# Dealing the second products of a two-layer network between its first products, with contiguous loads, later value loads and a factor moved into the exponent

## The chip, the cores and the metric

The kernel runs on one core of one Trainium2 chip. The metric is the device time of one execution in microseconds (us). Five engines take part: TensorE (PE; its weight loads are shown as PEld), VectorE (DVE), ScalarE (ACT), GpSimd (POOL) and SyncE (SP), which here only issues DMAs.

## The reference, cut to what matters

Blockwise causal attention for 8 batches of 8 heads, 576 tokens of 64 numbers each, then two matrix layers over the 4608 tokens. All of it is float32.

```python
scores = scale * np.matmul(q, k.transpose(0, 1, 3, 2))      # scale = 1/8
mask = block_i >= block_j                                   # blocks of 64 tokens
scores = np.where(mask, scores, -1000000000.0)
scores = scores - np.max(scores, axis=-1, keepdims=True)
attn = np.exp(scores)
attn = attn / (np.sum(attn, axis=-1, keepdims=True) + 1e-09)
x = np.matmul(attn, v)                                      # heads side by side: 4608 x 512
h = x @ w_in                                                # 512 -> 2048
g = np.maximum(0.01 * h, h)
out = g @ w_out                                             # 2048 -> 512
```

## The kernel before, in words

**Products in parts.** To keep float32 accuracy at the speed of the one-pass type float32r, an operand is split into a high part (rounded to float32r) and a low part (the rest), and three products are added: high with high, high with low, low with high. So `xh`, `xl` are the parts of x, `wih`, `wil` those of w_in, `gh`, `gl` those of g, `woh`, `wol` those of w_out. In the first heads a plain float32 product is used instead (`plain_s` for the scores, `plain_v` for the values), which takes four passes.

**Attention.** `attention(i)` makes one piece of work: a whole head for batches 1 to 7 ("full"), or for batch 0 the rows up to token 320 of a head ("lo", i = 0 to 7) and then the rest ("hi", i = 8 to 15). It loads q and k side by side into `qk_in` (two buffers) and the values into `vf`, or from batch 1 on into the one `v_stage`; forms scores in PSUM (`p_s`; in the odd lo heads `p_h`); takes masked row maxima, negated, into `nm` (L477); forms the exponents into `prow` with `nm` as the bias, and their sums (L486); divides by the sums; transposes `prow` through TensorE into `p_t` (L551) and copies it out; multiplies by the values (L603 or L613); and puts the result into `xr`. Where `plain_s` holds, q is first multiplied by the factor in place, in `qk_in` (by `copying`, L243 on ScalarE or L244 on VectorE).

**Weights.** `weight_piece` brings the 32 pieces of the two weight matrices, which arrive as 64-bit floats: a load into `raw`, two conversions, two bit operations that put a 32-bit value together in `val`, and the split into the two parts. A piece of w_out is 128 whole rows; a piece of w_in is a block of 128 columns.

**The two layers.** Tokens go in 18 chunks of 256. For each chunk the 2048 middle columns go in 8 pairs of column tiles, u = 0 to 7, so there are 144 pairs. `ffn1` makes the first products of a pair: for each of its two tiles 12 matmuls of 256 columns into `p_h[u % 2]`. Then ScalarE forms `g` from it (L719), which is split into `gh` and `gl` (two buffers each, by u % 2). `ffn2` makes the second products: for each half m of the chunk's tokens 6 matmuls of 512 columns into the accumulator `p_o[m]`. At u = 7 each accumulator is copied into the one buffer `ob` and stored.

**What sets the order.** Every step is given to `Plan.add` with the engines that could do it and their costs, a rank, and what it reads and writes. `Plan.run` plays the program through with these costs: each engine takes, of the steps whose inputs are there, the one of lowest rank. The order in which steps are taken is the program's order on each engine, and on SyncE's queue. Matmuls of one step stay together, so before the change the 12 first products of a tile are one block, and the 6 second products of a half another. The numbers at the head of the file shift ranks (`RL`: how many heads ahead q and k are loaded; `LEAD`, `LAG`: where first and second products stand among the heads; `OFF1`, `SL1`: when weight pieces are due), and `HOLD` is how long a step waits before its second-choice engine may take it. Until the first layer starts, where TensorE would rest in this play, dummy products of the identity (`fill`, L784, into `p_o`) are put in.

Of the kernel before, what the change touches and what calls it, by code (L numbers as in the profile page):

```python
# [26 lines left out]
HS = 8  # L27
SIGNS = 4
# [5 lines left out]
RL = 3.85  # L34
RP = 0.396
RB = 0.255
RT = 1.189
RV = 1.756
RX = -1.367
RN = -0.808  # L40

LEAD = 2.089
LAG = 1.994
RS = 2.992
RG = -0.004
OFF1 = 5.088
SL1 = 12.185
AHEAD = -0.653

LAT = 1550  # L50
HOLD = 167.582
# [6 lines left out]
SLOW = 8000  # L58
JOINT = 0


class Plan:
# [37 lines left out]
    def run(self):  # L100
# [123 lines left out]
def attention_ffn(ctx: ExitStack, tc: tile.TileContext, qk: bass.AP, v: bass.AP, w_in: bass.AP, w_out: bass.AP, out: bass.AP):  # L224
    nc = tc.nc
    B, H = qk.shape[0], qk.shape[1]
    DM, DFF = w_in.shape
# [65 lines left out]
    for y in range(2):  # L293
        nc.gpsimd.memset(sums[y], 1.0)
    xr = [fixed([P, ND, S], F32, "xr0"), None]
# [30 lines left out]
    def weight_piece(num, rank, f, out_side, c0):  # L326
# [31 lines left out]
        if src.dtype != F32:  # L358

            def load():  # L360
                nc.sync.dma_start(shaped(raws[k], 2 * P), src.bitcast(I32))
# [3 lines left out]
                ("ACT", act(w, True) + 70, lambda: nc.scalar.activation(val(), top(), AF.Copy, scale=2.0**-112)),  # L365
                ("DVE+", dve(w), lambda: nc.vector.tensor_scalar_mul(val(), top(), 2.0**-112)),
# [10 lines left out]
        else:  # L377

            def load():
                nc.sync.dma_start(shaped(val()), src)  # L380
# [5 lines left out]
    def attention(i):  # L386
# [25 lines left out]

        def load():
            if qa == 0:
                nc.sync.dma_start(qkt[:rows, :, :qe], qk[b, h, :rows, :, :qe])
            else:
                nc.sync.dma_start(qkt[:rows, 0, qa:qe], qk[b, h, :rows, 0, qa:qe])
                nc.sync.dma_start(qkt[:rows, 1, :ke], qk[b, h, :rows, 1, :ke])

        add([("SP", {"full": 475, "lo": 650, "hi": 1300}[kind], load)], r0 - RL, [], [qkey], lag=dma((qe - qa + ke) * rows * 4))  # L420
# [4 lines left out]
        add([("SP", 475, lambda: nc.sync.dma_start(vt(), v[b, h, :, :nv]))], r0 - RL + 0.1, [], [vkey], lag=dma(nv * P * D * 4))  # L425
# [389 lines left out]
```

## Time and profile before

| | |
|---|---|
| median of 3 runs | 1170.11 us (1169.79 to 1174.19) |
| the profiled execution | 1170.27 us |
| its span, first to last instruction | 1168.5 us |
| TensorE, share of the span | 99% |
| TensorE on the chain that ended last | 96% |
| first products begin | 50.36 us |

In the profile, rows in order of time give a start, a duration, the engine, the line, and what is written from what. A matmul's duration reaches from its start until its result is out, longer than the distance to the next start, since matmuls overlap. A float32 product of plain operands appears as two records. The table by stage gives for each stretch its length and each engine's busy time with the number of instructions in brackets. The chain that ended last is followed back from the last instruction: at each step to what released it, or to the instruction before it on its engine.

### The profile page before, as it was taken

The page shows a single profiled execution, that of the slowest core. Times are in us where ns is not written, and L with a number is a line of the kernel's source. Part 1 is how long each engine was busy: PE and PEld are TensorE (multiplying, and loading weights), DVE is VectorE, ACT ScalarE, POOL GpSimd, SP SyncE. Part 2 cuts the span into 40 slices and gives each one's busy share as a digit, 9 for nine tenths or more (in the row PEclk, how much of TensorE's full clock was granted, in tenths as well). Part 3 has the DMA queues.
Part 4 walks back from the last instruction along what each step waited for, and adds up shares of the span by engine and source line. Part 5 has one row for each costly group of instructions (what it writes and reads, how often), then busy time and mean ns, then how long its engine had stood idle before and what let it go on. Part 6 is the DMA issues. An engine that isn't in the chain of part 4 may idle for free.

```text
span 1168.5 us, 20725 instructions
## 1 busy us (share of the span) xinstructions
PE 1159.0 (99%) x7734; PEld 1053.7 (90%) x7734; DVE 622.7 (53%) x1606; ACT 649.0 (56%) x1641; POOL 432.8 (37%) x411
## 2 busy tenths in 40 slices
PE   8999999999999999999999999999999999999998
PEld 7878889899999999999999999999999999999997
DVE  6889988975555555535344555555555555200000
ACT  7888867765555555545455556565555555322222
POOL 2332444443443443434334344343343433222221
PEclk9999999999999999999999999999999999999999
DMA  7666322211212121111111111112111100000000
GB/s 225 218 220 229 124 67 79 87 62 53 71 47 70 33 70 53 66 32 60 38 45 47 50 53 65 41 51 64 52 65 52 54 29 25 2 19 3 16 19 19
DMA packets 38950, 78.16 MB, mean 67 GB/s; under 512 B 3520, under 2 KB 24000, under 8 KB 38848
## 3 DMA queue, kind: packets, MB, share of 16 engines
q1 hardware_dynamic: 38848, 76.82, 20.4%
q8 instruction: 61, 1.00, 0.3%
q14 instruction: 41, 0.34, 0.1%
HBM read 67.37 MB, written 9.44 MB: 66 GB/s over the span
## 4 chain that ended last, share of the span: by engine, by line
PE 96%; DVE 1%; DMA 1%; ACT 1%; issue 0%; SPq 0%; POOL 0%; ACTq 0%
PE p_h L712 34%; PE p_o L731 34%; PE p_t L551 9%; PE p_s L459 8%; PE p_t L613 7%; PE p_t L603 2%; PE p_s L453 2%; PE p_o L784 1%; PE p_h L453 0%; DMA qk_in<-in_qk 0%; DMA v_stage<-in_v 0%; DVE nm L477 0%; ACT prow L486 0%; DVE ptl L250 0%; DVE qs L436 0%
## 5 line engine op out<-in xcount | busy, mean ns | idle before, releaser
L712 PE MATMUL p_h<-xh,wih 128*128 128x256 f32 x1152 | 327.8, 285 | 0.0
L712 PE MATMUL p_h<-xl,wih 128*128 128x256 f32 x1152 | 321.1, 279 | 0.5 <-DVE xl L250 0.5
L712 PE MATMUL p_h<-xh,wil 128*128 128x256 f32 x1152 | 320.6, 278 | 0.0
L251 POOL TENSOR_TENSOR gl<-g,gh 128x512 fp32r<-128x512 f32 x138 | 181.1, 1312 | 298.5 <-ACT gh L240 199.2
L486 ACT ACTIVATE prow<-p_s,nm 128x192 f32<-128x192 f32 (+4 forms) x308 | 160.5, 527 | 139.7 <-DVE nm L477 137.2
L712 PEld LDWEIGHTS p_h<-xl,wih 128*128 128x128 f32 x1152 | 217.3, 189 | 8.6 <-DVE xl L250 0.8
L712 PEld LDWEIGHTS p_h<-xh,wih 128*128 128x128 f32 x1152 | 216.7, 188 | 8.1 <-issue 0.4
L712 PEld LDWEIGHTS p_h<-xh,wil 128*128 128x128 f32 x1152 | 216.9, 188 | 0.0
L719 ACT ACTIVATE g<-p_h 128x512 f32<-128x512 f32 x144 | 85.6, 595 | 213.4 <-PE p_h L712 202.1
L517 POOL TENSOR_SCALAR prow<-prow,rec 128x576 f32<-128x576 f32 (+3 forms) x121 | 88.0, 730 | 310.3 <-DVE rec L505 282.6
L731 PE MATMUL p_o<-woh,gh 128*128 128x512 f32 x576 | 183.3, 399 | 0.0
L731 PE MATMUL p_o<-woh,gl 128*128 128x512 f32 x576 | 179.4, 393 | 0.0
L731 PE MATMUL p_o<-wol,gh 128*128 128x512 f32 x576 | 179.3, 393 | 0.0
L477 DVE TENSOR_REDUCE nm<-p_s 128x1 f32<-128x192 f32 (+4 forms) x308 | 140.1, 486 | 4.7
L551 PE MATMUL p_t<-ident,prow 128*128 128x128 f32 x960 | 130.2, 273 | 1.2 <-DVE xr L592 0.5
L731 PEld LDWEIGHTS p_o<-woh,gl 128*128 128x128 f32 x576 | 108.2, 188 | 24.3
L731 PEld LDWEIGHTS p_o<-wol,gh 128*128 128x128 f32 x576 | 108.2, 188 | 23.9
L250 DVE TENSOR_TENSOR ptl<-p_t,pth 128x512 fp32r<-128x512 f32 (+1 forms) x224 | 118.8, 567 | 16.8 <-ACT pth L240 14.3
L551 PEld LDWEIGHTS p_t<-ident,prow 128*128 128x128 f32 x960 | 110.0, 141 | 12.6 <-issue 1.9
L592 DVE TENSOR_TENSOR xr<-p_t,xr 64x64 f32<-64x64 f32 x112 | 50.2, 449 | 126.8 <-ACT xr L240 121.6
L240 ACT CAST pth<-p_t 128x384 fp32r<-128x384 f32 (+3 forms) x190 | 86.1, 499 | 39.8 <-PE p_t L551 39.6
L251 POOL TENSOR_TENSOR kl<-qk_in,kh 128x576 fp32r<-128x576 f32 x55 | 85.3, 1551 | 22.5 <-ACT kh L240 17.9
(78 smaller groups left out, 1561.7 us busy)
## 6 DMA issues: line engine op xcount, KB each, us to landing
qk_in<-in_qk SPq DMA_DIRECT2D x56, 576.0 KB, 3.7
v_stage<-in_v SPq DMA_DIRECT2D x56, 160.0 KB, 2.2
out<-ob SPq DMA_DIRECT2D x35, 256.0 KB, 2.3
raw<-in_w_in SPq DMA_DIRECT2D x16, 512.0 KB, 4.6
raw<-in_w_out SPq DMA_DIRECT2D x16, 512.0 KB, 3.9
qk_in<-in_qk SPq DMA_DIRECT2D x8, 320.0 KB, 4.0
qk_in<-in_qk SPq DMA_DIRECT2D x8, 288.0 KB, 3.7
vf<-in_v SPq DMA_DIRECT2D x8, 160.0 KB, 3.2
```

The lines of the kernel that those rows point to most:

```text
L240: one = lambda: nc.scalar.copy(dst(), src())
L250: ("DVE+" if sb else "DVE", dve(n), lambda: nc.vector.tensor_sub(dst(), one(), two())),
L251: ("POOL", pool2(n), lambda: nc.gpsimd.tensor_sub(dst(), one(), two())),
L459: go = lambda ap=ap, cols=cols, kk=kk, k0=k0, k1=k1, first=first, last=last: nc.tensor.matmul(ap, qs[z][:, cols], kk[:, k0:k1], start=firs ...
L477: [("DVE", dve(kw[t]), lambda t=t, ap=ap, flat=flat: nc.vector.tensor_reduce(nm[z][: qn[t], t : t + 1], ap[: qn[t]], axis=AX.X if flat els ...
L486: nc.scalar.activation(o, ap[: qn[t]], AF.Exp, bias=nm[z][: qn[t], t : t + 1], scale=1.0, accum_out=sums[z][: qn[t], t : t + 1])
L517: ("POOL", pool1(kw[t]), lambda: nc.gpsimd.tensor_scalar(p(), p(), by, 1.0, op0=ALU.mult, op1=ALU.mult)),
L551: return 27, lambda: nc.tensor.transpose(p_t[x][:, c : c + n], row(t, n, j * P, P), ident[:n, :n])
L613: nc.tensor.matmul(to, vs[z][:, j, :], src, start=start, stop=stop)
L712: nc.tensor.matmul(hh[:, i, :], w[:, d, f * P : (f + 1) * P], x[:, d, :], start=k == 0, stop=k == len(terms) - 1)
L719: add([("ACT", act(512), lambda: nc.scalar.activation(g, hh, AF.Prelu, alpha=0.01))], rank, [("h", z)], ["g"])
L731: nc.tensor.matmul(p_o[m], a[:, i, m * P : (m + 1) * P], w[:, 2 * u + i, :], start=u == 0 and k == 0, stop=u == NU - 1 and k == 5,)
```

## The change

1. **Second products dealt.** From u = 2 on, `ffn1` no longer makes a block of 12 first products. It takes the second products of pair u - 2 of the same chunk and deals them in: one second product, two first products, and so on. Tile i of the pair goes with half m = i. Each tile is two steps of 9 matmuls. Pairs 0 and 1 have their first products alone, and at u = 7 `ffn2` adds the second products of pairs 6 and 7, undealt.
2. **The plan.** A matmul step that depends on another matmul step no longer waits in the plan for that one's end.
3. **Contiguous loads.** w_in is laid out on the host so that a piece is 128 whole rows of 4 KB. q and k of batch 0 come from an array of their own, `qk0`, in which the columns of a lo or hi piece stand side by side, so each needs one load with one run per partition.
4. **Later value loads.** They get rank `r0 - RL + VD` with VD = 5.23, about 0.57 heads ahead of their head instead of 3.75.
5. **Factor in the exponent.** With `plain_s`, q is not multiplied. The exponent takes the factor as its `scale`, and the negated maxima in `nm` are multiplied by it, in one small step per group of rows.
6. **Choices.** The conversion of a weight's top word may run on GpSimd. HS goes from 8 to 7, so one hi head forms its scores from parts. The table of ranks, and HOLD, have other values.

```diff
-HS = 8
+HS = 7
-RL = 3.85
+RL = 5.803
...
-HOLD = 167.582
+HOLD = 62.559
...
+VD = 5.23
...
-                at = max([0] + [ends[d][1] + self.SYNC.get((ends[d][0], e), 0) for d in self.ops[i][2]])
+                at = max([0] + [ends[d][1] + self.SYNC.get((ends[d][0], e), 0) for d in self.ops[i][2] if (ends[d][0], e) != ("PE", "PE")])
...
-            src = w_in[c0 : c0 + WIDE, fs].rearrange("(c p) f -> p c f", p=P)
+            src = w_in[f, :, c0 : c0 + WIDE]
...
+                ("POOL", pool1(w), lambda: nc.gpsimd.tensor_scalar(val(), top(), 2.0**-112, 1.0, op0=ALU.mult, op1=ALU.mult)),
...
-        add([("SP", 475, lambda: nc.sync.dma_start(vt(), v[b, h, :, :nv]))], r0 - RL + 0.1, [], [vkey], lag=dma(nv * P * D * 4))
+        add([("SP", 475, lambda: nc.sync.dma_start(vt(), v[b, h, :, :nv]))], r0 - RL + VD, [], [vkey], lag=1.5 * dma(nv * P * D * 4))
...
-            add(copying(qe - qa, lambda: q_in, lambda: q_in, by=scale / 2), rp, [], [qkey])
...
+            if plain_s:
+                ts = sorted(t for t, _, _ in tiles)
+                some = nm[z][:, ts[0] : ts[-1] + 1]
+                add([
+                    ("DVE+", 75, lambda some=some: nc.vector.tensor_scalar_mul(some, some, scale / 2)),
+                    ("ACT", 110, lambda some=some: nc.scalar.activation(some, some, AF.Copy, scale=scale / 2)),
+                ], r, [], [("nm", z, t) for t in ts])
...
-                    o, ap[: qn[t]], AF.Exp, bias=nm[z][: qn[t], t : t + 1], scale=1.0, accum_out=sums[z][: qn[t], t : t + 1]
+                    o, ap[: qn[t]], AF.Exp, bias=nm[z][: qn[t], t : t + 1], scale=scale / 2 if plain_s else 1.0, accum_out=sums[z][: qn[t], t : t + 1]
...
+    def ffn1(c, u, rank, rank0):
+        z = u % 2
+        mate = u - 2 if u >= 2 else None
         for i in range(2):
...
+            one = ffn1_terms(u, i)
+            if mate is None:
+                add([("PE", one)], rank + i / 1000, xkeys + wkeys[("wi", 2 * u + i)], [("h", z)])
+                continue
+            two = ffn2_terms(mate, i)
+            for y in range(2):
+                a, b = one[6 * y : 6 * y + 6], two[3 * y : 3 * y + 3]
+                mixed = [x for k in range(3) for x in (b[k], a[2 * k], a[2 * k + 1])]
+                add(
+                    [("PE", mixed)], rank + i / 1000 + y / 2000,
+                    xkeys + wkeys[("wi", 2 * u + i)] + ffn2_keys(mate), [("h", z), ("o", i)], kind="long",
                 )
...
     def ffn2(c, u, rank):
         for m in range(2):
+            if u == NU - 1:
+                for x in (u - 1, u):
+                    add([("PE", ffn2_terms(x, m))], rank + m / 1000 + (x - u) / 300, ffn2_keys(x), [("o", m)], kind="long")
```

On TensorE, in the middle of the program, the end of a block of first products (`p_h`) and the blocks of second products (`p_o`, one accumulator for each half) behind it stand like this before (x2 is two instructions of that form):

```order
L712 MATMUL p_h_109<-xh,wih 128x256
L712 MATMUL p_h_109<-xl,wih 128x256
L712 MATMUL p_h_109<-xh,wil 128x256
L731 MATMUL p_o_110<-woh,gh_114 128x512 x2
L731 MATMUL p_o_110<-wol,gh_114 128x512 x2
L731 MATMUL p_o_110<-woh,gl_116 128x512 x2
L731 MATMUL p_o_111<-woh,gh_114 128x512 x2
L731 MATMUL p_o_111<-wol,gh_114 128x512 x2
L731 MATMUL p_o_111<-woh,gl_116 128x512 x2
```

And now, at the like place, with the last triple of one pair and the first three of the next:

```order
L733 MATMUL p_o_113<-woh,gl_117 128x512
L721 MATMUL p_h_110<-xl,wih 128x256
L721 MATMUL p_h_110<-xh,wil 128x256
L733 MATMUL p_o_112<-woh,gh_116 128x512
L721 MATMUL p_h_111<-xh,wih 128x256
L721 MATMUL p_h_111<-xl,wih 128x256
L733 MATMUL p_o_112<-woh,gh_116 128x512
L721 MATMUL p_h_111<-xh,wil 128x256
L721 MATMUL p_h_111<-xh,wih 128x256
L733 MATMUL p_o_112<-wol,gh_116 128x512
L721 MATMUL p_h_111<-xl,wih 128x256
L721 MATMUL p_h_111<-xh,wil 128x256
```

Runs of 12 first and 6 second products have become rows in which every second product stands alone between two pairs of first products.

On SyncE's queue, at the program's start, the loads of q and k (`qk_in`), values (`vf`) and weights (`raw`) before:

```order
L415 DMA qk_in_86<-in_qk 128x2x320
L425 DMA vf_130<-in_v 128x256
L415 DMA qk_in_87<-in_qk 128x2x320
L425 DMA vf_131<-in_v 128x256
L361 DMA raw_123<-in_w_in 128x4x256
```

And now:

```order
L425 DMA qk_in_86<-in_qk 128x640
L425 DMA qk_in_87<-in_qk 128x640
L432 DMA vf_132<-in_v 128x256
L432 DMA vf_133<-in_v 128x256
L363 DMA raw_125<-in_w_in 128x1024
```

Both loads of q and k have moved ahead of the values, and each has one run per partition.

On ScalarE, at the program's start, with the factor on q (L243), a weight's conversions (L365, L368) and the exponents (L486), before:

```order
L243 ACT_TABLE_LOAD
L243 ACTIVATE qk_in_86<-qk_in_86 128x320
L243 ACTIVATE qk_in_87<-qk_in_87 128x320
L365 ACTIVATE val_126<-raw_123 128x512
L368 ACTIVATE raw_123<-raw_123 128x512
L486 ACTIVATE prow_2_75,sums_98<-p_s,nm_96 128x320
```

And now, with other line numbers (L367 and L371 are the conversions, L499 the exponents):

```order
L367 ACT_TABLE_LOAD
L367 ACTIVATE val_128<-raw_125 128x512
L499 ACTIVATE prow_2_75,sums_98<-p_s,nm_96 128x320
L499 ACTIVATE prow_1_74,sums_98<-p_s,nm_96 128x192
L499 ACTIVATE prow_0_73,sums_98<-p_s,nm_96 64x64
L371 ACTIVATE raw_125<-raw_125 128x512
```

The two instructions that multiplied q are gone; one conversion now runs ahead of the first exponents instead of two. Until the first products of the layers, TensorE's order has 64 dummy products where it had 59. On ScalarE, counted to its first `g`, 8 instructions on `qk_in` are gone, 8 on `nm` have come, and conversions of a weight's top word are 6 instead of 10; GpSimd has 6 of these conversions ahead of its first `gl`.

More of the change, by code (lines that the diff above doesn't have):

```diff
@@ L32 @@
 VALS = 3
-RL = 3.85
[L35 to L48, printed above, removed]
+RL = 5.803
+RP = 0.25
+RB = 0.531
+RT = 1.509
+RV = 1.966
+RX = -3.191
+RN = -0.618
+LEAD = 2.353
+LAG = 2.006
+RS = 1.957
+RG = -0.335
+OFF1 = 4.843
+SL1 = 10.955
+AHEAD = -1.469
 LAT = 1550
-HOLD = 167.582
+HOLD = 62.559
 FILL = 235
@@ L379, in load @@
             def load():
-                nc.sync.dma_start(shaped(val()), src)
+                nc.sync.dma_start(val(), src)
             add([("SP", 475, load)], rank - AHEAD, [], [v_key], lag=dma(w * P * 4))
@@ L453, in scores @@
                     go = lambda ap=ap, cols=cols, k0=k0, k1=k1, first=first, last=last: nc.tensor.matmul(
-                        ap, qkt[:rows, 0, cols], qkt[:rows, 1, k0:k1], start=first, stop=last
+                        ap, q_in[:, cols.start - qa : cols.stop - qa], k_in[:, k0:k1], start=first, stop=last
                     )
@@ new lines, in ffn2_terms, with go @@
+    def ffn2_terms(u, m):
+        z = u % 2
+        terms = [(a, w, i) for a, w in ((gh[z], woh), (gh[z], wol), (gl[z], woh)) for i in range(2)]
+        def go(k):
+            a, w, i = terms[k]
+            nc.tensor.matmul(
+                p_o[m], a[:, i, m * P : (m + 1) * P], w[:, 2 * u + i, :],
+                start=u == 0 and k == 0, stop=u == NU - 1 and k == 5,
+            )
+        return [(RATE * DM, lambda k=k: go(k)) for k in range(6)]
+    xkeys = [(a, d) for a in ("xh", "xl") for d in range(0, CH, BLK)]
@@ L718, in ffn1 @@
         rank += RG
-        add([("ACT", act(512), lambda: nc.scalar.activation(g, hh, AF.Prelu, alpha=0.01))], rank, [("h", z)], ["g"])
+        add([("ACT", act(512), lambda: nc.scalar.activation(g, p_h[z], AF.Prelu, alpha=0.01))], rank, [("h", z)], ["g"])
         add(copying(512, lambda: gh[z], lambda: g), rank, ["g"], [("gh", z)])
@@ L723, in ffn2 @@
     def ffn2(c, u, rank):
-        z = u % 2
         for m in range(2):
-            terms = [(a, w, i) for a, w in ((gh[z], woh), (gh[z], wol), (gl[z], woh)) for i in range(2)]
-            def go(k, m=m, terms=terms):
-                a, w, i = terms[k]
-                nc.tensor.matmul(
-                    p_o[m], a[:, i, m * P : (m + 1) * P], w[:, 2 * u + i, :],
-                    start=u == 0 and k == 0, stop=u == NU - 1 and k == 5,
-                )
-            add(
-                [("PE", [(RATE * DM, lambda k=k, go=go: go(k)) for k in range(6)])], rank + m / 1000,
-                [("gh", z), ("gl", z)] + wkeys[("wo", 2 * u)] + wkeys[("wo", 2 * u + 1)], [("o", m)], kind="long",
-            )
+            if u == NU - 1:
+                for x in (u - 1, u):
+                    add([("PE", ffn2_terms(x, m))], rank + m / 1000 + (x - u) / 300, ffn2_keys(x), [("o", m)], kind="long")
             if u == NU - 1:
```

60 lines of the change are left out of this document (36 added, 24 removed).

## The prediction

> **What bounds the kernel now.** The profile's page was read first: engines, slices, chain. Then a table by stage, then rows in order of time.
>
> ```profile
> span 1168.5 us, 20725 instructions
> PE 1159.0 (99%) x7734; PEld 1053.7 (90%) x7734; DVE 622.7 (53%) x1606; ACT 649.0 (56%) x1641; POOL 432.8 (37%) x411
> PEclk9999999999999999999999999999999999999999
> PE 96%; DVE 1%; DMA 1%; ACT 1%; issue 0%; SPq 0%; POOL 0%; ACTq 0%
> L712 PE MATMUL p_h<-xh,wih 128*128 128x256 f32 x1152 | 327.8, 285 | 0.0
> L731 PE MATMUL p_o<-woh,gh 128*128 128x512 f32 x576 | 183.3, 399 | 0.0
> ```
>
> TensorE carries 96% of the chain, at full granted clock, and the largest groups have no idle time before them. The mean of one instruction (285 and 399 ns) is no price: matmuls overlap, so I price by the distance between starts. There are three groups like the first and three like the second: 144 column pairs make 3456 first products of 256 columns and 1728 second products of 512. One second and two first products, a triple, are the unit below; there are 1728 triples.
>
> Busy time by stage (TensorE, weight loads, VectorE, ScalarE, GpSimd, then clock and DMA share):
>
> ```profile
> 0.00:50.00 50.00, 46.76 (x285) 38.48 (x286) 36.38 (x107) 39.84 (x113) 9.85 (x26) 1.00 0.71 223
> 50.00:250.00 200.00, 197.49 (x1297) 173.12 (x1296) 174.34 (x418) 159.18 (x385) 85.84 (x83) 1.00 0.41 132
> 250.00:1010.00 760.00, 760.00 (x5159) 701.89 (x5158) 403.25 (x1068) 411.14 (x1078) 303.31 (x277) 1.00 0.16 51
> ```
>
> From 250 us on TensorE never rests and VectorE and ScalarE are half idle: there only the spacing of matmuls can move the time. Before 50 us no product of the layers has run; ScalarE (80%), VectorE (73%) and the loads (0.71) set the pace, and TensorE fills its waits with dummy products. The chain of this stage and the group of the dummies:
>
> ```profile
> 2.08 5.09 DMA qk_in<-in_qk
> 7.20 0.48 ACT qk_in L243
> 7.72 2.40 PE p_h L453 x6
> 46.51 1.98 PE p_o L784 x16
> ...
> 50.36 1.42 PE p_h L712 x12
> L784 PE MATMUL p_o<-ident 128*128 128x128 f32 x117 | 18.5, 308 | 1.4 <-POOL ident masks.py:199 1.4
> ```
>
> **The dealing of second products.** How matmuls follow one another now, in the tail, where attention is over:
>
> ```profile
> 1037.20 0.62 PE L731 MATMUL p_o<-woh,gl 128*128 128x512 f32 x2
> 1037.66 0.28 PE L712 MATMUL p_h<-xh,wih 128*128 128x256 f32 x1
> 1037.77 0.28 PE L712 MATMUL p_h<-xl,wih 128*128 128x256 f32 x1
> 1037.89 0.28 PE L712 MATMUL p_h<-xh,wil 128*128 128x256 f32 x1
> 1038.01 0.28 PE L712 MATMUL p_h<-xh,wih 128*128 128x256 f32 x1
> 1038.13 0.28 PE L712 MATMUL p_h<-xl,wih 128*128 128x256 f32 x1
> 1038.25 0.28 PE L712 MATMUL p_h<-xh,wil 128*128 128x256 f32 x1
> ...
> 1038.93 0.28 PE L712 MATMUL p_h<-xh,wil 128*128 128x256 f32 x1
> 1039.04 0.62 PE L731 MATMUL p_o<-woh,gh 128*128 128x512 f32 x2
> 1039.50 0.62 PE L731 MATMUL p_o<-wol,gh 128*128 128x512 f32 x2
> ```
>
> Second products are 0.46/2 = 230 ns apart. The twelve first products take 1039.04 - 1037.66 = 1.38 us, 115 ns each, but not evenly: the first five after a second product take 0.59 us (118 ns each), and the six from 1038.25 to 1038.93 take 0.68 us (113 ns each). A triple costs 230 + 2 x 115 = 460 ns.
>
> In a dealt row every first product stands within two of a second product, so the fast steps deep in a run are not reached. I take the first three steps of the run, 1037.66 to 1038.01, 117 ns each: 230 + 2 x 117 = 464 ns. Only pairs 2 to 7 of a chunk are dealt: 18 chunks x 6 pairs x 12 = 1296 triples. The term is 1296 x 4 ns = +5.2 us.
>
> Its ends: downwards, both first products at the 113 ns of the deep run, 230 + 226 = 456 ns, -5.2 us. Upwards, another run of before, which never left the slow spacing:
>
> ```profile
> 500.00 0.28 PE L712 MATMUL p_h<-xl,wih 128*128 128x256 f32 x1
> ...
> 502.00 0.63 PE L731 MATMUL p_o<-woh,gh 128*128 128x512 f32 x2
> 502.46 0.63 PE L731 MATMUL p_o<-wol,gh 128*128 128x512 f32 x2
> 502.93 0.62 PE L731 MATMUL p_o<-woh,gl 128*128 128x512 f32 x2
> ```
>
> Seventeen first products in 2.00 us are 118 ns each, and the second products behind them 0.93/4 = 232 ns. With the largest step of the fast run (1038.01 to 1038.13, 120 ns) a triple is 232 + 240 = 472 ns: +15.6 us. The middle value is nearest to the rows where the two kinds meet.
>
> The Trainium skill, page "TensorE: Matmul & The Clock Gate", section "Back-to-back issue gap", gives columns / 2.4 + about 2.5 ns between matmuls, 109 and 216 ns here, and the part on loading the stationary operand says that loading the next weights takes no read bandwidth from the running matmul. By that an undisturbed triple would be 434 ns. The rows above contradict it in both kinds; it is a rival below.
>
> The moved instructions issue no DMA. In each dealt block a wait for the halves of g now holds first products behind it. They are two pairs old by then, some 24 triples or 11 us, against one activation, one copy and one subtraction of about 0.6, 0.6 and 1.3 us:
>
> ```profile
> L719 ACT ACTIVATE g<-p_h 128x512 f32<-128x512 f32 x144 | 85.6, 595 | 213.4 <-PE p_h L712 202.1
> L251 POOL TENSOR_TENSOR gl<-g,gh 128x512 fp32r<-128x512 f32 x138 | 181.1, 1312 | 298.5 <-ACT gh L240 199.2
> ```
>
> So I price it at nothing; were half a pair late by 1 us in each of the 108 dealt pairs, it would cost 108 us, which is why the wait's cover matters. At a chunk's end in the tail the next chunk's first dealt row follows the last second products at once, and the accumulator of the second half is free only after the first half's copy, its store, and a second copy through the same `ob`:
>
> ```profile
> L240 ACT COPY ob<-p_o x33: 577/587/594, 145.0 to 1163.4; 128x512 f32<-128x512 f32 x33
> DMA to landing us min/median/max: 2.0/2.3/4.2
> ```
>
> The store starts about 0.6 us before the last second product ends, lands 2.3 us after it is issued, and the copy takes 0.6 us: some 2.7 us in all with the issue, against 6 triples x 464 = 2.8 us of cover. I take +0.2 us at each of four chunk ends, +0.8 us (0 to +4 by the slowest landing).
>
> **The first 50 us.** The factor on q is gone. On the chain it stood as 0.48 us, and the second head's load is now issued ahead of both value loads: I take -0.9 us (ends -0.5, the activation alone, and -2.0). In place of the factor each softmax scales the negated maxima, a column or three, between maximum and exponent. The nearest rows for the saving and for the addition:
>
> ```profile
> L243 ACT ACTIVATE qk_in<-qk_in 128x320 f32<-128x320 f32 (+1 forms) x8 | 3.6, 453 | 4.7 <-DMA qk_in<-in_qk 4.7
> L365 ACT ACTIVATE val<-raw 128x512 f32<-128x512 f32 x9 | 6.0, 664 | 1.4 <-DMA raw<-in_w_in 1.4
> L502 DVE TENSOR_SCALAR rec<-sums 128x3 f32<-128x3 f32 (+1 forms) x8 | 1.2, 156 | 0.1
> ```
>
> Eight factors of 0.45 us leave ScalarE (3.6 us), eight scalings at about 0.2 us (an estimate from the last row and a little more for ScalarE) come (1.6 us), and four conversions of a weight's top word move to GpSimd, busy for 9.9 of these 50 us (2.7 us). Against 4.7 us saved stands a weight schedule that asks for one to two pieces more in the same time. I take half, -2.3 us (0 to -4.7). If the scaling's 0.2 us are not covered by the other head of the pair, 16 of them cost +3.2 us. The order has 64 dummies where it had 59; by the chain's 1.98 us for 16 records, two records each, +1.2 us (0 if they only fill waits).
>
> Contiguous loads and later value loads: the two sides of the weights load equal bytes, one in pieces of 1 KB, one in whole rows.
>
> ```profile
> raw<-in_w_in SPq DMA_DIRECT2D x16, 512.0 KB, 4.6
> raw<-in_w_out SPq DMA_DIRECT2D x16, 512.0 KB, 3.9
> ```
>
> So a piece lands up to 0.7 us sooner, on loads that are issued several heads ahead: nothing on the chain, 16 x 0.7 = -11 us if each were waited for. The Trainium skill ("DMA: Bandwidth & Descriptors", Specifications) has transfers of 512 B or more at line rate, by which the rearranging would save nothing at all; the 0.7 us speak for a small gain in latency. One of the 64 heads no longer runs its scores in four-pass float32:
>
> ```profile
> 48.49 0.75 PE p_s L453 x2
> 54.17 0.97 PE p_s L453 x4
> ```
>
> These are 1.72 us for a head; split into parts, it saves between nothing and all of it, I take -0.9 us.
>
> **Sum.** The profiled execution took 1170.27 us, its span 1168.5. The span: 1168.5 + 5.2 + 0.8 - 0.9 - 2.3 + 1.2 - 0.9 = 1171.6; with the 1.8 us around it 1173.4, 3.1 us above a median of 1170.11, which this execution all but equals. I forecast 1173 us. A measurement of this kernel can tell about 0.5% from no change, 5.9 us: below 1164.3 is faster, above 1176.0 slower.
>
> **Rivals.** (a) Dealing keeps the deep run's spacing, and the first stage gives its full gain: 456 ns a triple, -5.2 instead of +5.2, and -2.4 more from ScalarE, -1.2 without the dummies' term: about 1159 us. For it: 113 ns exist, and a first product before a second one has them. Against: the five steps behind every second product. Chance 0.24. (b) The slow spacing becomes the rule, the other side of no change: 472 ns, 10.4 us more than forecast, 1184 us. It decides from 466 ns on. For it: a run of 24 that never recovered, with slow second products behind it. Against: most runs did recover. Chance 0.22. (c) The added scaling lengthens the chain of maximum and exponent in the first stage, and the earlier weights take ScalarE's room: +3.2 and +2.3, 1179 us, chance 0.06. (d) Matmuls are slowed only by neighbours of their own kind, so that dealing frees both: by the shortest single step of the rows, 110 ns twice with 230 ns, a triple is 450 ns, 14 below the forecast's, 18.1 us, 1155 us. The page's undisturbed 434 ns would give 1134 us. No run of steps in the rows speaks for it; chance 0.05. (e) Nothing on the chain changes: 1170, within the forecast's own reach.
>
> **How the numbers follow.** The forecast and (e) hold 0.43, and reach from 1164 to 1180 by half of the distance to the mixing term's ends and all of that to the first stage's. Faster is (a) but for a little, (d), and the lower edge of the forecast: 0.22 + 0.05 + 0.08 = 0.35. Slower is (b), (c) in part, and the upper edge: 0.21 + 0.04 + 0.03 = 0.28. The rest, 0.37, is the same. The range leaves out (d) and the ends of (a) and (b): 1155 to 1187.
>
> **What would show it.** In the tail of the changed profile, starts in order of time: 230 then two steps of 117 ns would bear out the main term; 113 says (a), 118 to 120 with 232 says (b). The table by stage should still show TensorE without rest from 250 us on; idle time before `p_o` or `p_h` released by GpSimd or ScalarE would mean that the wait for g's halves is not covered, and the forecast wrong in a way that no rival prices. The first product of the layers should start at 47 to 51 us, against 50.4 now, and the dummies' group should hold 128 records.

## The result, and the profile after

| | before | after |
|---|---|---|
| median of 4 runs each | 1169.95 us (1169.49 to 1174.19) | 1180.13 us (1180.03 to 1180.70) |
| span of the profiled execution | 1168.5 us | 1178.9 us |

The ratio is 1.008, with a 95% interval of 1.0067 to 1.0092: the change made the kernel slower, by 10.2 us.

The profile's page of the changed kernel (busy us, share of the span, instructions; then groups with busy us and mean ns of one, and the idle time before them):

```profile
span 1178.9 us, 20564 instructions
PE 1170.3 (99%) x7744; PEld 1064.4 (90%) x7744; DVE 688.7 (58%) x1733; ACT 631.2 (54%) x1591; POOL 365.6 (31%) x346
PEclk9999999999999999999999999999999999999999
L721 PE MATMUL p_h<-xh,wih 128*128 128x256 f32 x1152 | 324.5, 282 | 0.0
L733 PE MATMUL p_o<-woh,gh 128*128 128x512 f32 x576 | 221.6, 405 | 0.0
```

TensorE is still the bound, at full clock, and its busy time grew by 11.3 us, the span by 10.4. The mean of one second product of the row shown is 405 ns where it was 399, and that of a first product fell from 285 to 282, so these means mislead: the cost shows only in the distances between starts. The table by stage says in which stage TensorE rested (its busy time is the first number behind the length):

```profile
0.00:50.00 50.00, 47.63 (x305) 39.14 (x306) 38.88 (x102) 38.46 (x117) 18.67 (x36) 1.00 0.73 240
50.00:250.00 200.00, 197.53 (x1295) 174.70 (x1294) 173.44 (x423) 159.51 (x390) 71.72 (x70) 1.00 0.40 127
250.00:1010.00 760.00, 760.00 (x5103) 702.12 (x5102) 462.87 (x1187) 393.49 (x1019) 244.25 (x217) 1.00 0.16 51
```

It rests nowhere after 250 us, and before that as little as it did (2.5 us between 50 and 250 us, then and now). So the 10 us went into the matmuls themselves. And this is what TensorE waited for, as engine, line, releaser: us in total, times, longest:

```profile
PE p_t L564 <- ACT prow L532: 1.7, 2, 1.5
PE p_o L816 <- POOL ident masks.py:199: 1.4, 1, 1.4
PE p_s L458 <- DMA qk_in<-in_qk: 0.6, 1, 0.6
PE p_s L464 <- ACT prow L499: 0.6, 2, 0.4
PE p_h L721 <- DVE xl L251: 0.2, 1, 0.2
PE p_t L564 <- DVE prow L531: 0.2, 1, 0.2
```

Neither `gh`, `gl` nor `ob` is in the list: the halves of g are never late for a dealt row, and the chunk ends hold nothing up.

The start, in order of time (chain rows, then rows of TensorE) and the dummies:

```profile
0.74 2.86 DMA qk_in<-in_qk
3.64 2.39 PE p_s L458 x6
...
49.15 1.39 PE p_h L721 x12
```

```profile
48.10 1.05 PE L816 MATMUL p_o<-ident 128*128 128x128 f32 x8
48.91 0.37 PE L721 MATMUL p_h<-xh,wih 128*128 128x256 f32 x1
```

```profile
L816 PE MATMUL p_o<-ident 128*128 128x128 f32 x128 | 17.8, 286 | 1.4 <-POOL ident masks.py:199 1.4
```

The scores of the first head now start on the load itself, without the factor between, and the first product of the layers starts at 48.91 us. The 50.36 us given for before is from the chain, where the first block now stands at 49.15 us, so it is 1.2 us sooner.

The tail, where the main term of the prediction was to be read:

```profile
1045.61 0.40 PE L733 MATMUL p_o<-woh,gh 128*128 128x512 f32 x1
1045.85 0.28 PE L721 MATMUL p_h<-xh,wil 128*128 128x256 f32 x1
1045.97 0.28 PE L721 MATMUL p_h<-xh,wih 128*128 128x256 f32 x1
1046.09 0.40 PE L733 MATMUL p_o<-wol,gh 128*128 128x512 f32 x1
1046.32 0.28 PE L721 MATMUL p_h<-xl,wih 128*128 128x256 f32 x1
1046.44 0.28 PE L721 MATMUL p_h<-xh,wil 128*128 128x256 f32 x1
1046.56 0.40 PE L733 MATMUL p_o<-wol,gh 128*128 128x512 f32 x1
...
1049.40 0.40 PE L733 MATMUL p_o<-woh,gh 128*128 128x512 f32 x1
```

From 1045.61 to 1049.40 there are eight triples: 3.79 / 8 = 474 ns each. The first product follows the second by 0.24 us (239 ns in most rows), the two steps behind it are 0.12 us each (117 and 118 ns). The tail's runs of before gave 460 ns.

**An account of TensorE's time.** For this and the tables below I added up, over all matmuls of a trace, the distance from each start to the next, by kind. Time with no matmul running is counted as idle. One thing needs care: the last transposition of a block of attention shows a start only 28 or 29 ns ahead of what follows, which then takes 313 ns instead of 231. To keep the kinds apart, a product right behind attention's or a dummy matmul is entered at 117 ns (first) or 230 ns (second), and the rest goes to attention.

| us | first products | second products | both | attention | dummies | idle | ends |
|---|---|---|---|---|---|---|---|
| before, 1168.5 | 400.6 | 398.2 | 798.8 | 343.2 | 16.6 | 4.4 | 5.5 |
| after, 1178.9 | 405.4 | 405.5 | 810.9 | 342.9 | 16.1 | 3.5 | 5.5 |
| difference | +4.8 | +7.3 | +12.1 | -0.3 | -0.5 | -0.9 | 0.0 |

The 5184 products cost 12.1 us more, and all else together 1.7 us less. By its neighbours, a second product between two first ones takes 237.2 ns in the mean of 1111 (median 239), against 230.0 ns between two of its like in before (mean of 1204). At the two borders of a run of before it took 229.0 and 230.9 ns.

### The profile page after: what moved, and what is told of

Its sections match the earlier page's. It is cut to its first block, busy times and chain, and to the rows that moved or that the text cites. A ratio compares the mean times of both kernels' runs of the same rounds, so it can differ in the third digit from the quotient of the medians.

```text
span 1178.9 us, 20564 instructions
## 1 busy us (share of the span) xinstructions
PE 1170.3 (99%) x7744; PEld 1064.4 (90%) x7744; DVE 688.7 (58%) x1733; ACT 631.2 (54%) x1591; POOL 365.6 (31%) x346
## 4 chain that ended last, share of the span: by engine, by line
PE 95%; DVE 2%; ACT 1%; issue 0%; DMA 0%; DVEq 0%; ACTq 0%
PE p_h L721 34%; PE p_o L733 33%; PE p_t L564 9%; PE p_t L626 8%; PE p_s L464 7%; PE p_t L616 1%; PE p_s L458 1%; PE p_o L816 1%; ACT prow L499 1%; DVE val L376 0%; PE p_h L458 0%; DVE qs L441 0%; DVE nm L482 0%; DVE prow L531 0%; DMA qk_in<-in_qk 0%
## 5 line engine op out<-in xcount | busy, mean ns | idle before, releaser
L721 PE MATMUL p_h<-xh,wih 128*128 128x256 f32 x1152 | 324.5, 282 | 0.0
L252 POOL TENSOR_TENSOR gl<-g,gh 128x512 fp32r<-128x512 f32 x110 | 143.6, 1306 | 472.8 <-ACT gh L241 321.5
L499 ACT ACTIVATE prow<-p_s,nm 128x192 f32<-128x192 f32 (+4 forms) x308 | 159.6, 524 | 142.5 <-DVE nm L482 138.1
L733 PE MATMUL p_o<-wol,gh 128*128 128x512 f32 x576 | 222.3, 406 | 0.0
L733 PE MATMUL p_o<-woh,gh 128*128 128x512 f32 x576 | 221.6, 405 | 0.0
L733 PE MATMUL p_o<-woh,gl 128*128 128x512 f32 x576 | 217.5, 398 | 0.0
L564 PE MATMUL p_t<-ident,prow 128*128 128x128 f32 x960 | 134.8, 273 | 2.0 <-ACT prow L532 1.7
L733 PEld LDWEIGHTS p_o<-woh,gh 128*128 128x128 f32 x576 | 105.9, 188 | 3.2
L252 POOL TENSOR_TENSOR kl<-qk_in,kh 128x576 fp32r<-128x576 f32 x52 | 76.4, 1469 | 41.8 <-ACT kh L241 29.6
L242 DVE CAST pth<-p_t 128x512 fp32r<-128x512 f32 (+3 forms) x95 | 57.4, 634 | 51.4 <-PE p_t L564 49.9
L464 PE MATMUL p_s<-kh,qs 128*128 128x192 f32 (+1 forms) x339 | 85.6, 311 | 0.6 <-ACT prow L499 0.6
```

What stands on the lines that cost most here:

```text
L242: two = lambda: nc.vector.tensor_copy(dst(), src())
L252: ("POOL", pool2(n), lambda: nc.gpsimd.tensor_sub(dst(), one(), two())),
L464: go = lambda ap=ap, cols=cols, kk=kk, k0=k0, k1=k1, first=first, last=last: nc.tensor.matmul(ap, qs[z][:, cols], kk[:, k0:k1], start=firs ...
L499: nc.scalar.activation(o, ap[: qn[t]], AF.Exp, bias=nm[z][: qn[t], t : t + 1], scale=scale / 2 if plain_s else 1.0, accum_out=sums[z][: qn ...
L564: return 27, lambda: nc.tensor.transpose(p_t[x][:, c : c + n], row(t, n, j * P, P), ident[:n, :n])
L721: nc.tensor.matmul(hh[:, i, :], w[:, d, f * P : (f + 1) * P], x[:, d, :], start=k == 0, stop=k == len(terms) - 1)
```

## The experiments

The theory: the dealt order itself costs the time, whatever feeds it, because a second product alone between first ones takes longer and the first ones never reach their fast step. The rival: the order of the plan, the ranks or the loads cost it, and the spacing is a by-product. Later runs ask what in the dealing costs: the length of the matmuls, the number of changes from one kind to the other, or the change of operands and accumulator. (Where an expectation has letters, A is the theory, and a number behind it one of these readings.) Ratios are to the kernel before, run on the same chip, with 95% intervals; "products" and "idle" are those of the account above, made for each kernel:

| kernel | second : first in a row | span | products | attention | dummies | idle |
|---|---|---|---|---|---|---|
| before | runs of 6 and 12 | 1168.5 | 798.8 | 343.2 | 16.6 | 4.4 |
| after | 1 : 2 | 1178.9 | 810.9 | 342.9 | 16.1 | 3.5 |
| e2_runs | 3 : 6 | 1166.7 | 799.5 | 342.8 | 16.1 | 2.7 |
| e1_undealt | runs of 6 and 12 | 1173.8 | 798.7 | 345.3 | 16.0 | 8.3 |
| e3_dealt_before | 1 : 2 | 1194.7 | 813.5 | 346.7 | 17.6 | 11.4 |
| e4_halves | runs of 12 halves and 12 | 1172.8 | 799.2 | 344.9 | 16.0 | 7.4 |
| e5_tile_runs | 6 : 12 | 1188.2 | 801.2 | 349.3 | 16.5 | 15.7 |
| e6_two_four | 2 : 4 | 1195.6 | 808.0 | 350.5 | 16.6 | 15.0 |
| e7_pair_runs | 12 : 24 | 1237.6 | 798.5 | 369.5 | 16.7 | 47.4 |
| e10_loads_split | 3 : 6 | 1169.2 | 800.0 | 342.8 | 16.3 | 4.6 |
| e8_factor_on_q | 3 : 6 | 1182.2 | 801.3 | 347.7 | 18.6 | 9.1 |
| e9_values_early | 3 : 6 | 1181.4 | 800.6 | 347.7 | 18.2 | 9.3 |
| e11_dealt_halves | 2 halves : 2 | 1179.4 | 812.5 | 342.4 | 16.1 | 3.0 |
| e12_old_ranks | runs of 6 and 12 | 1174.5 | 799.5 | 343.1 | 18.4 | 8.1 |

Two things have to be kept in mind with this table. Runs e1 to e4 were measured on one chip, e5 to e12 on another. And in the traces of some kernels TensorE's granted clock was 0.50 for stretches of 3.4 us, or a few such in a row, mostly in the first 260 us: 3.4 us in all in e1, e3, e4 and e12, 13.7 in e5, e8 and e9, 17.1 in e6, 44.4 in e7, and none before the last 2 us in before, after, e2, e10 and e11. A matmul takes nearly twice as long there. So part of what the table gives as attention, and 1 to 4 us of the products of e3 to e9 and e12, is not spacing but the clock.

**The order inside a step alone (e2_runs).** The changed kernel, with the same steps of nine matmuls at the same places, but in each the three second products first and then the six first ones. No other engine's order differs.

```diff
-                mixed = [x for k in range(3) for x in (b[k], a[2 * k], a[2 * k + 1])]
+                mixed = b + a
```

> The changed kernel with every dealt step of nine matmuls in another inner order: its 3 second products first, then its 6 first products. No other engine's order changes. Theory A: three second products at about 230 to 233 ns, then five slow first products (592 ns together, as the kernel before has behind second products) and one at 114 ns, so about 467 ns a triple and 1171 us (1166 to 1174). Rival B: about 1180 us, since the steps, their order and their waits are the same.

Measured: 1168.56 us (1168.10 to 1169.23), ratio 0.997 (0.9957 to 0.9983); the span is 12.2 us below that of after, and 11.4 us of it are the products. The tail:

```profile
1046.17 0.62 PE L733 MATMUL p_o<-woh,gh 128*128 128x512 f32 x2
1046.63 0.39 PE L733 MATMUL p_o<-wol,gh 128*128 128x512 f32 x1
1046.86 0.28 PE L721 MATMUL p_h<-xh,wih 128*128 128x256 f32 x1
1046.98 0.28 PE L721 MATMUL p_h<-xl,wih 128*128 128x256 f32 x1
...
1047.45 0.28 PE L721 MATMUL p_h<-xh,wil 128*128 128x256 f32 x1
1047.57 0.39 PE L733 MATMUL p_o<-wol,gh 128*128 128x512 f32 x1
```

Three triples from 1046.17 to 1047.57 take 1.40 us, 467 ns each; the three second products take 0.46 + 0.23 us, 230 ns each, the last of them with a first product behind it. The theory is borne out: the same matmuls, in the same steps, cost 11 us more when dealt one to two. This kernel is faster than after, and by 0.3% faster than before.

**Dealing undone, all else kept (e1_undealt).**

```diff
-        mate = u - 2 if u >= 2 else None
+        mate = None
...
-            if u == NU - 1:
-                for x in (u - 1, u):
-                    add([("PE", ffn2_terms(x, m))], rank + m / 1000 + (x - u) / 300, ffn2_keys(x), [("o", m)], kind="long")
+            add([("PE", ffn2_terms(u, m))], rank + m / 1000, ffn2_keys(u), [("o", m)], kind="long")
```

> The changed kernel with first and second products in runs again, as before the change (12 first products of a tile, 6 second products of a half); everything else of the change stays. Theory A (the loss is the spacing of dealt matmuls: 239 ns for a second product and 117.5 ns for a first one, 474 ns a triple, against 460 ns in clean runs and some 463 ns on the average of the kernel before, on 1296 triples): 1162 to 1166 us, second products back at 229 ns. Rival B (the loss is in the rest: other order, waits, first stage): it stays at about 1180 us.

Measured: 1173.54 us (1172.12 to 1175.62), ratio 1.0022 (1.0013 to 1.0031). The expectation missed by 7.5 us. The products did fall by 12.2 us, to those of before, but 4.8 us more of idle time and 2.4 us more in attention took over half of it back. The plan came out anew on all engines, and TensorE waits more; 2 us of attention's part lie in the stretch from 13.9 us on in which the clock was 0.50. That the ranks, chosen for the dealt steps, do not suit blocks of another length is a guess, which e12 below does not bear out.

**Dealing alone, on the kernel before (e3_dealt_before).** `ffn1` and `ffn2` of the changed kernel and the plan's rule for matmul behind matmul, with ranks, loads and factor of before.

```diff
+        mate = u - 2 if u >= 2 else None
...
+                mixed = [x for k in range(3) for x in (b[k], a[2 * k], a[2 * k + 1])]
```

> The kernel before with the dealing alone (and the plan's rule that a matmul step doesn't wait for another one's end, which the dealing needs); loads, factor and ranks as before. Theory A: 1296 triples at 474 ns instead of 460 to 463, 1184 to 1188 us. Rival B (dealing costs nothing by itself): about 1170 us.

Measured: 1196.63 us (1196.50 to 1198.70), ratio 1.0226 (1.0213 to 1.0240), 8 us or more above what was expected. The products account for 14.7 us against before; the rest is idle time (+7.0), attention (+3.5) and dummies (+1.0). The stage in which it rests:

```profile
50.00:250.00 200.00, 190.91 (x1221) 166.35 (x1220) 166.43 (x394) 152.19 (x364) 77.03 (x72) 0.99 0.40 129
```

TensorE rests for 9.1 us here, against 2.5 in before. The dealt steps under the old ranks make TensorE wait; which of the ranks does it was not tried.

**Old ranks with runs (e12_old_ranks).** e1 with the ranks and HOLD of before. With RL = 3.85, VD = 3.28 keeps the value loads 0.57 heads ahead, as in the changed kernel:

```diff
-LEAD = 2.353
-LAG = 2.006
+LEAD = 2.089
+LAG = 1.994
...
-VD = 5.23
+VD = 3.28
```

> The undealt kernel (loads, factor, value loads and choices of the change) with the ranks of the kernel before. If the other parts gain the 2 to 5 us that the first stage shows in the changed kernel, and the undealt kernel lost them by ranks made for dealt steps: 1165 to 1168 us. If the parts gain nothing without the new ranks: 1169 to 1172 us. If these parts need the new ranks: over 1173 us.

Measured: 1175.73 us (1173.82 to 1177.47), ratio 1.0038 (1.0025 to 1.0051). The products are those of before; idle time (8.1) and dummies (18.4) are not. The old ranks, under which before ran in blocks of these same lengths, gain nothing under the new parts: e12 is no faster than e1. Without dealing, the new parts are slower than before under either table, and why is open.

**Is it the length? (e4_halves, e11_dealt_halves).** Each second product of 512 columns becomes two of 256 with the same weights, so that all matmuls of the layers are equally long; in e4 on e1's runs, in e11 in dealt rows of two halves and two first products.

```diff
+            cols = slice(256 * y, 256 * y + 256)
...
-                p_o[m], a[:, i, m * P : (m + 1) * P], w[:, 2 * u + i, :],
+                p_o[m][:, cols], a[:, i, m * P : (m + 1) * P], w[:, 2 * u + i, cols],
```

> As the undealt kernel, but each second product of 512 columns is made as two of 256 columns with the same weights, so that all matmuls of the two layers are of one length. Theory A1 (matmuls of one length fall into step with their weight loads, 113 ns each, and the slow steps come from the change of length): second products cost 2 x 113 = 227 ns instead of 229, and the 27 ns of slow steps behind each run of second products go, 288 times: 8 to 12 us under the undealt kernel. Theory A2 (every weight load takes 10 to 16 ns from the matmul beside it, whatever stands next to it): 2 x (107 + 10 to 16) = 234 to 246 ns a second product, 9 to 29 us over the undealt kernel.

Measured: 1173.99 us (1172.78 to 1174.60), ratio 1.0025 (1.0015 to 1.0035), the same as e1. Products 799.2 against 798.7: two halves cost what one whole costs, and neither the gain nor the loss that was expected came.

> The changed kernel, dealt one to two as it is, but each second product of 512 columns made as two of 256 with the same weights, so that all matmuls are of one length while operands and accumulators still change. Theory A1 (the change of length makes matmuls slow): all go at 113 to 118 ns, 452 to 472 ns a triple instead of 474 to 476, 1150 to 1176 us. Theory A4 (the change of operands or accumulator makes them slow): four matmuls at 118 to 124 ns, 475 ns a triple or more, 1180 to 1200 us.

Measured: 1182.21 us (1181.15 to 1183.58), ratio 1.0088 (1.0071 to 1.0106), the same as after. Rows of its tail:

```profile
1060.03 0.40 PE L734 MATMUL p_o<-woh,gl 128*128 128x256 f32 x2
1060.27 0.28 PE L721 MATMUL p_h<-xl,wih 128*128 128x256 f32 x1
1060.38 0.28 PE L721 MATMUL p_h<-xh,wil 128*128 128x256 f32 x1
1060.50 0.40 PE L734 MATMUL p_o<-woh,gh 128*128 128x256 f32 x2
...
1061.45 0.40 PE L734 MATMUL p_o<-wol,gh 128*128 128x256 f32 x2
```

Three groups in 1.42 us are 473 ns each, as in after. With all matmuls equally long the loss is still there: a mixture of lengths is not its cause. What is left of the readings tried is the change of kind, that is of operands and accumulator. This is argued by exclusion; which of the two it is, no run here tells.

**How often the kind changes (e5_tile_runs, e6_two_four).** One step per tile, in e5 the six second products and then the twelve first ones, in e6 two and four in turn. The two have the same steps at the same ranks.

```diff
-            for y in range(2):
-                a, b = one[6 * y : 6 * y + 6], two[3 * y : 3 * y + 3]
...
+            add(
+                [("PE", two + one)], rank + i / 1000,
```

> The changed kernel with one step per tile: 6 second products, then the tile's 12 first products, still of pairs two apart. Theory A (slow steps only near a change of kind): 6 second products at 229 ns, five slow first products (592 ns) and seven at 113 ns, 460 ns a triple: 18 us less than the changed kernel's 474 on 1296 triples, 4 to 6 us less than with runs of 3 and 6, so 1162 to 1165 us, unless the coarser steps make attention wait. Rival B: 1180.

Measured: 1191.05 us (1190.01 to 1192.69), ratio 1.0176 (1.0160 to 1.0192). Missed by over 25 us: the products are good (801.2), but TensorE waits (idle 15.7, attention +6.1 against before, some 4 us of it at half clock). The likely reason is that a step of 18 matmuls holds attention's short ones up, and with them what attention should have set going.

```diff
-                [("PE", two + one)], rank + i / 1000,
+                [("PE", [x for k in range(3) for x in two[2 * k : 2 * k + 2] + one[4 * k : 4 * k + 4]])], rank + i / 1000,
```

> The same steps and the same order of steps on every engine as with one step per tile, but inside a step two second products and four first ones in turn. If a matmul is slow only at a change of kind (cost per change): half of the dealt loss, 464 to 467 ns a triple, 5 to 9 us over one step per tile. If it takes five matmuls of a kind to get out of the slow spacing (theory A3: a slow phase that only a long run leaves): 474 ns a triple as in the changed kernel, 18 us over one step per tile.

Measured: 1197.27 us (1193.71 to 1197.66), ratio 1.0219 (1.0201 to 1.0236), 6.2 us above e5; the products are 6.8 us above. In its tail:

```profile
1063.53 0.64 PE L733 MATMUL p_o<-wol,gh 128*128 128x512 f32 x2
1064.00 0.28 PE L721 MATMUL p_h<-xl,wih 128*128 128x256 f32 x1
...
1064.36 0.28 PE L721 MATMUL p_h<-xl,wih 128*128 128x256 f32 x1
1064.47 0.64 PE L733 MATMUL p_o<-woh,gl 128*128 128x512 f32 x2
```

Two triples in 0.94 us, 470 ns each, at full clock. With the table: 1 : 2 costs 810.9, 2 : 4 costs 808.0, 3 : 6 costs 799.5, and from 6 : 12 on it is 798.5 to 801.2. Against the 798.7 of e1, 1 : 2 costs 12.2 us for 1296 groups, 9 ns each, and 2 : 4 costs 9.3 us for 648 groups, 14 ns each; without the 2 us that the half clock adds there, some 7 us, 11 ns each. So the whole price falls with the number of changes, though one change costs no less, until at three and six (432 groups, 0.8 us) it is all but gone. The account by kind tells more: in e1, e6 and after the first products take 400.8, 408.7 and 405.4 us, the second ones 397.9, 399.3 and 405.5. With two second products together theirs is nearly the price of a run; what e6 still loses is in its first products, which in groups of four stay at 117 to 119 ns and never reach 113. So there are two losses, and groups of two end only the first.

**One step per pair (e7_pair_runs).** Twelve second products, then 24 first ones, in one step.

```diff
+            row = [x for m in range(2) for x in ffn2_terms(mate, m)] + [x for i in range(2) for x in ffn1_terms(u, i)]
+            add(
+                [("PE", row)], rank,
```

> The changed kernel with one step per pair: 12 second products, then 24 first products. Theory A: 12 x 229 + 592 + 19 x 113 ns, 457 to 458 ns a triple, 3 us less than one step per tile, 1159 to 1163 us. Rival: steps of 5.5 us hold up attention's matmuls, the engines behind them run dry in the first 250 us, and it is slower than one step per tile.

Measured: 1241.10 us (1237.17 to 1247.26), ratio 1.0609 (1.0584 to 1.0634). The rival of this run was right:

```profile
50.00:250.00 200.00, 178.25 (x1044) 151.83 (x1043) 147.53 (x339) 128.70 (x306) 55.56 (x53) 0.91 0.36 114
250.00:1010.00 760.00, 742.89 (x4996) 680.48 (x4995) 496.10 (x1235) 388.14 (x993) 210.13 (x176) 1.00 0.17 53
```

```profile
PE p_s L464 <- ACT prow L499: 8.7, 8, 2.3
PE p_t L564 <- DVE xr L605: 7.2, 6, 2.1
```

TensorE rests for 22 us between 50 and 250 us, where the granted clock fell to 0.91, and for 17 us more after; the two largest sums of its waits, shown here, are for softmax and for attention's results. The products are the cheapest of all, 798.5 us, but idle time (+43.9 us against after) and attention (+26.6, of which some 17 lie in stretches at half clock) lose nearly six times the 12 us that the dealing had cost.

**The loads of before (e10_loads_split).** e2 with w_in in pieces of 1 KB, and q and k of batch 0 with two runs per partition or in two loads; on TensorE, VectorE, ScalarE and GpSimd the order is e2's.

```diff
-            src = w_in[f, :, c0 : c0 + WIDE]
+            src = w_in[c0 : c0 + WIDE, fs].rearrange("(c p) f -> p c f", p=P)
...
-                nc.sync.dma_start(qf[:, : nq + ke], qk0[h, :, o : o + nq + ke])
+                nc.sync.dma_start(qkt[:rows, :, :qe], qk[b, h, :rows, :, :qe])
```

> The kernel with runs of 3 and 6 and the loads of before: w_in in pieces of 1 KB, q and k of batch 0 in two runs per partition or two loads; the order on every engine is kept. If contiguous loads only shorten transfers that nothing waits for: the same as with runs of 3 and 6, 1168.6 us within 1 us. If the first 130 us wait for loads: 2 to 11 us more.

Measured: 1171.04 us (1168.96 to 1172.32), ratio 1.0002 (0.9991 to 1.0012), 2.5 us above e2, or 3.7 by the ratios, since e2 ran on the other chip. The spans of the two traces differ by 2.5 us. The first issues on SyncE's queue in e2:

```profile
0.74 0.85 SPq L425 DMA_DIRECT2D qk_in<-in_qk  x2
1.64 0.90 SPq L432 DMA_DIRECT2D vf<-in_v  x2
2.58 0.43 SPq L363 DMA_DIRECT2D raw<-in_w_in  x1
```

and in e10:

```profile
0.74 1.30 SPq L418 DMA_DIRECT2D qk_in<-in_qk  x2
2.09 1.07 SPq L430 DMA_DIRECT2D vf<-in_v  x2
3.20 0.43 SPq L363 DMA_DIRECT2D raw<-in_w_in  x1
```

A load of q and k with one run takes 0.43 us to issue, one with two runs 0.65 us. The value loads, which are the same in both, took 0.45 and 0.54 us each. So the first weights start 0.62 us later. They also land later: this is the time from issue to landing of the first two pieces of w_in, in e2 and in e10:

```profile
DMA to landing us min/median/max: 5.0/5.8/6.7
DMA to landing us min/median/max: 6.2/7.0/7.9
```

The first piece, with 5.0 and 6.2 us, is thus there 1.8 us later, ScalarE waits 1.8 us longer for it (7.4 us instead of 5.6), and the first product of the layers starts at 50.66 us instead of 48.92. Over all 16 pieces the median landing is 4.2 us here and 4.3 us in e2, so whole rows gained nothing there. The Trainium skill, page "DMA: Bandwidth & Descriptors", section "Specifications", has transfers of 512 B or more at line rate. In the median landing the trace agrees; packet by packet it does not quite, with 46 ns for 1024 B and 159 ns for 4096 B, 22 against 26 GB/s. That the 2.5 us come from the first pieces, a third by the issue and two thirds by the landing, is argued from these rows; the pieces of w_in and the loads of q and k were not split apart.

**Factor and value loads (e8_factor_on_q, e9_values_early).** e2 with q multiplied again, and e2 with the values loaded right behind q and k, 5.7 heads ahead (before had 3.75); in both the plan was made anew.

```diff
+            add(copying(nq, lambda: q_in, lambda: q_in, by=scale / 2), rp, [], [qkey])
...
-                    o, ap[: qn[t]], AF.Exp, bias=nm[z][: qn[t], t : t + 1], scale=scale / 2 if plain_s else 1.0, accum_out=sums[z][: qn[t], t : t + 1]
+                    o, ap[: qn[t]], AF.Exp, bias=nm[z][: qn[t], t : t + 1], scale=1.0, accum_out=sums[z][: qn[t], t : t + 1]
```

> The kernel with runs of 3 and 6, but q multiplied by the factor in place as before, instead of the factor in the exponent and on the maxima. If the forecast's terms hold (0.9 us at the start, and half of 4.7 us of ScalarE in the first 50 us): 1 to 5 us slower than with the factor in the exponent, 1170 to 1173 us. Rival (the small steps on the maxima lengthen each softmax by as much): the same, 1168 to 1169 us, or up to 3 us faster.

Measured: 1184.15 us (1180.32 to 1186.90), ratio 1.0104 (1.0080 to 1.0129), 15.6 us above e2.

```diff
-VD = 5.23
+VD = 0.1
```

> The kernel with runs of 3 and 6, but value loads right behind the loads of q and k, 5.7 heads ahead in rank. If value loads of the first stage take the place of loads that are waited for, or stop SyncE's queue while they wait for their buffer: 1 to 5 us slower. If nothing waits for them either way: the same, 1168 to 1169 us.

Measured: 1181.17 us (1179.50 to 1183.17), ratio 1.0075 (1.0055 to 1.0095), 12.6 us above e2. Two edits that have nothing in common lose nearly the same, and in the same way: 6.4 and 6.6 us of idle time, 4.9 us each in attention, 2.5 and 2.1 us of dummies. Two of the waits of e8, in the last brackets (us and releaser):

```profile
223.55 0.80 PE L465 MATMUL p_s<-kh,qs 128*128 128x448 f32 x2 [1.53 <-ACT prow L492]
...
230.52 1.73 PE L557 MATMUL p_t<-ident,prow 128*128 128x128 f32 x7 [1.48 <-DVE xr L598]
```

These lie far behind the heads on which the factor works. They also cost twice: right behind them the granted clock was 0.50 (the last but two number) from 223.0 to 236.7 us,

```profile
223.10:236.60 13.50, 11.39 (x43) 9.97 (x44) 9.68 (x24) 7.71 (x22) 4.98 (x5) 0.50 0.17 56
```

and in e9, behind waits of 1.52, 0.50 and 1.53 us at the same place, from 225.4 to 235.6. The matmuls of attention in these stretches (in e9 with another one at 13.8 us) took some 5 us more than at full clock, which is all of the 4.9 us. Each edit made the plan come out otherwise on all engines, so neither run prices its part; what the factor and the value loads are worth by themselves stays open.

## Why the prediction was right or wrong, point by point

**The dealing: the direction right, the size wrong, in the second product.** The measured 1180.1 us lie within the range, but above the 1176.0 us from which the prediction calls a kernel slower, and it gave slower 0.28, less than faster (0.35) or the same (0.37). The way was right; of 10.2 us only 3.1 were forecast (3.3 above the median; the 3.1 are above the profiled execution). The step that failed is "230 + 2 x 117 = 464 ns": it took the 230 ns of a second product among its like for one that stands alone between first products. Those cost 239 ns in the steady rows and 237.2 in the mean of all; no row of before could show it, since at the borders of its runs second products took 229.0 and 230.9 ns, as inside. The other half of the step was right: first products kept the slow 117 to 118 ns, and cost 4.8 us more where +5.2 was forecast. That it came so near is in part luck: two first products took 235.4 ns where 234 was forecast, and over the whole of before they had taken 231.8, not the 230 of the tail. The second products' +7.3 us, forecast at nothing, are as much as the span missed its forecast by (1171.6 to 1178.9).

**Rivals.** (a) fell: 113 ns occurs only in undealt runs. (b) had nearly the price, 472 ns, and the sign, from the slow spacing of one long run; but its steps (232 ns, and the slowest first step twice) are not the ones that came (239, 117, 118). Its 1184 us was nearer than my 1173, and came out too high because it added the slow steps to a base of 460 ns that held in the tail alone. Over the whole of before a triple took 2 x 115.9 + 230.6 = 462.4 ns. (d) fell with (a): dealing slows the second product instead of freeing it; and its step of 110 ns was a rounding of the view, since the first step of such a run is 117 ns in the trace (median of 89 runs). The formula that the Trainium skill's "Back-to-back issue gap" (page "TensorE: Matmul & The Clock Gate") gives for an isolated matmul, and by which a triple would have been 434 ns, agrees with no run here: 462 in runs, 474 dealt. (c) is not seen: TensorE's waits ahead of 50 us became shorter, not longer. (e), no change at all, fell too.

**The wait for g's halves, priced at nothing.** Right: no row among TensorE's waits names `gh` or `gl`.

**Chunk ends, +0.8 us.** Nothing of it is seen; `ob` is not waited for.

**The first stage and attention.** Forecast: -0.9 for the chain, -2.3 for ScalarE, +1.2 for dummies, -0.9 for one head, +0.8 for chunk ends, -2.1 us together. Measured: -0.9 idle, -0.5 dummies, -0.3 attention, -1.7 us. The sum came near, but that is no proof of its parts: there are 128 records of dummies, as the order said, but they cost less time than the 117 of before, not 1.2 us more, and e8, which was to price the factor, could not. The first product came at 48.91 us, within the 47 to 51 forecast.

**Contiguous loads, priced at nothing on the chain.** Too low: e10 gives 2.5 us, by the start of the first product 1.7 us. The prediction took the pieces as issued several heads ahead and so waited for by nobody. For the first piece of w_in that is not so: ScalarE waits for it, and it came 1.8 us later with the loads of before.

**Not in the prediction:** how much idle time a new plan can bring, and what the clock adds to it. It did not bear on this change (idle 3.5 us, clock 1.00), but on nearly every experiment in which the plan came out anew.

## What to carry to other kernels

Price a matmul by the distance to the next start, and price it between the neighbours that it will have: a run of its like says nothing about one that stands alone, so measure one row of the new order before an interleaving is trusted. Interleave in groups of three and six or more where it has to be done: in this kernel e2 keeps all that the finer steps of the plan gave and loses only 0.7 us of the spacing against before. Where a planner's ranks are tuned, undoing one part makes the whole order come out anew, so compare kernels whose order on the other engines is the same (as e2 and e10), or count idle time and spacing apart, as in the account above, and look at the granted clock before a longer time is put down to the order.

## What the runs showed of the hardware that was not expected

- A matmul of 512 columns takes 230 ns behind and ahead of its like and 239 ns alone between others with another operand and accumulator; two of 256 columns in its place cost the same, 473 ns a group against 474.
- One of 256 columns has two steps, 113 to 114 and 117 to 118 ns. Behind second products a run begins in the slow one and mostly drops to the fast one after five matmuls (117, 117, 118, 122, 118, then 113 in before); some runs stay in the slow one to their end (500 us into before, and the tail of e4). What decides it was not found.
- Behind waits of TensorE of some 1.5 us and more, alone or added up over a few us, its granted clock fell to 0.50 for 3.4 us or a few times that; in e8 (217 to 224 us) no single one was longer than 1.54 us. But the same length did not always do it: one wait of 1.52 us at 10.5 us in e1 was followed by such a stretch, one of 1.52 us at 111.7 us in after was not. From 50 to 250 us in e7 the mean is 0.91, and attention's matmuls took 369.5 us in all instead of 342.8. In before, after and e2, where TensorE rested for 1.7 to 2.5 us in the same 200 us, it stayed at 1.00.
